# Matmuls in place of transposes as fillers of TensorE's first gaps

## The chip, the core and the metric

The kernel runs on one core of a Trainium2 chip. Its time is the device time in microseconds (us) of one execution, and of several executions the median is given. The engines are called by their short names: PE (TensorE, matmuls), ACT (ScalarE), DVE (VectorE), POOL (GpSimd) and SP, whose queue here issues the transfers.

## What is computed

Two parts in a row: a block-wise linear attention with decay, over 4 batches, 8 heads, 768 tokens and 64 dimensions, and a two-layer network with a leaky ReLU over the 3072 tokens of 512 features that come out of it.

```python
for b in range(nb):                       # blocks of 64 tokens
    qb, kb, vb = (q[:, :, sl], k[:, :, sl], v[:, :, sl])
    intra = np.einsum('bhic,bhjc->bhij', qb, kb) * Dmask[None]
    intra = np.einsum('bhij,bhjd->bhid', intra, vb)
    inter = np.einsum('bhid,bhde->bhie', qb * lam_pow[None], kv_state)
    out[:, :, sl] = intra + inter
    kb_dec = kb * rev_pow[None]
    kv_state = lam_block * kv_state + np.einsum('bhsd,bhse->bhde', kb_dec, vb)
...
x = attn_out.transpose(0, 2, 1, 3).reshape(B * S, H * D)     # 3072 x 512
h = x @ w_in                                                 # w_in 512 x 2048
return np.maximum(0.01 * h, h) @ w_out                       # w_out 2048 x 512
```

The weights `w_in` and `w_out` come as 64-bit floats and are turned into 32-bit ones on the chip.

## The kernel before

The tokens go in 24 chunks of 128 (`c`), and four chunks form a group of 512 (`g`). A chunk takes these steps: loads of k, q and v; transposes of k and q on PE against an identity (line 404) into PSUM, copied out by ACT (lines 415 and 416); the small 64x64 matmuls of scores, state and output (all in the helper `quad`, line 314); elementwise work on DVE and POOL between them (lines 420 to 463); and the split of the attention's output into three float32r parts, high, low and mixed (`xh`, `xl`, `xm`, lines 508 to 511). The three parts are held in `X[g % 2]`, so `X[1]` belongs to group 1 first. When a group is whole, the first layer multiplies it with the weights' three parts (`product`, line 641): 512-column float32r matmuls, four for each partial product. After all groups comes the second layer (line 701).

All work is added to a planner, `Plan`, with an engine, an estimated duration and the keys that it reads and writes. `emit` orders the operations by their estimated times and ranks, and then issues them in that order, so each engine's queue is fixed when the kernel is built. While it issues, `emit` also follows a second estimate of the time. Where PE would stand idle for more than 0.4 us by this estimate, it calls `self.idle(n)` with a number of fillers that is reckoned from the gap:

```python
if self.spare in self.ops[i][4]:
    self.idle = None
if self.idle is not None and t > soon[e] + 0.4:
    self.idle(int((t - soon[e] - 0.2) / 0.16))
```

It stops for good at the first operation that writes the bank `b10` (`spare`), which is the first 512-column matmul of the first layer. Until then the bank is free, and the fillers write their results there; nobody reads them. In the kernel before, `plan.idle` is `busy`: `n` transposes of the 128x128 identity with itself, in 32-bit floats (line 267). The same `busy` gives the eleven transposes that PE starts with (`WARM`), before the first data are there. The identity, `ident`, is made by POOL at the start. Fillers stand in PE's queue like other matmuls: what is behind them in the queue starts after them.

Of the kernel before, what the change touches and what calls it, by code (L numbers as in the profile page):

```python
# [31 lines left out]
def _bc(ap, idx, n):  # L32
    a = [list(x) for x in ap.ap]
    return bass.AP(ap.tensor, ap.offset, a[:idx] + [[0, n]] + a[idx:])
# [129 lines left out]
def kernel(  # L164
# [10 lines left out]
    nc = tc.nc  # L175
    P = 128
# [10 lines left out]
    T = GC * C  # L187
    WARM = 11
# [22 lines left out]
    def sb(shape, name, dt=F32):  # L211
        return pool.tile(shape, dt, name=name, tag=name)

    def ps(shape, name):
        return psum.tile(shape, F32, name=name, tag=name)
# [5 lines left out]
    b1, b2 = [ps([P, T], f"b1{i}") for i in range(2)], ps([P, T], "b2")  # L221
# [3 lines left out]
    X = [[sb([P, KO, T], f"x{x}{i}", F32R) for x in "hlm"] for i in range(2)]  # L225
# [14 lines left out]
    def part(n):  # L240
        nonlocal used
        used += n
        assert used <= NA, used
        return att[:, used - n:used]

    ident = part(P)
# [13 lines left out]

    nc.scalar.dma_start(out=lam_b, in_=lam.partition_broadcast(P))
    make_identity(nc, ident)

    def busy(n):

        for _ in range(n):
            nc.tensor.transpose(out=b1[0][:, 0:P], in_=ident, identity=ident)

    busy(WARM)
    nc.gpsimd.memset(zero, 0.0)  # L270
    plan = Plan()
    plan.idle, plan.spare, plan.warm = busy, "b10", 1.3 + 0.22 * WARM
    add = plan.add
    steady = False

# [546 lines left out]
```

## Time and profile before

| | us |
|---|---|
| median of three runs | 611.7 |
| runs | 611.04, 611.7, 614.07 |
| profiled execution, its time | 611.24 |
| profiled execution, its span | 609.4 |
| PE busy, share of the span | 598.5, 98% |
| DVE busy | 312.4 |
| ACT busy | 268.5 |
| POOL busy | 86.4 |

The span goes from the first to the last instruction of the profiled execution; its time holds some 2 us around it besides. PE's busy time contains matmuls that overlap: the record of one lasts longer than the distance to the next one. Lines such as L267 are those of the kernel before. In the kernel after, `busy` stands at line 269 and the new matmul at line 274, and all lines behind `hold` are 8 higher.

### The profile page before, as it was taken

What the parts mean: (1) busy time and instruction counts of PE and PEld (TensorE: products, weight loads), DVE (VectorE), ACT (ScalarE), POOL (GpSimd) and SP (SyncE); (2) the same over time, 40 slices, a digit from 0 to 9 for tenths busy, and PEclk for the clock granted to TensorE, in tenths of its full rate; (3) what the DMA queues carried; (4) which work ended last, traced back from release to release, by engine and by line L of the source; (5) the groups of instructions that cost most, each with busy time, mean ns of one, the idle gap of its engine ahead of it and who ended that gap; (6) DMA issues with size and microseconds to landing.
All of it is one profiled execution on the core that took longest, in us unless ns stands there. A gap on an engine that the chain in (4) does not pass through costs nothing.

```text
span 609.4 us, 12970 instructions
## 1 busy us (share of the span) xinstructions
PE 598.5 (98%) x5406; PEld 495.5 (81%) x5406; DVE 312.4 (51%) x417; ACT 268.5 (44%) x428; POOL 86.4 (14%) x91
## 2 busy tenths in 40 slices
PE   8899999999999999999999999999999999999997
PEld 6687888888888888888788888888888888888886
DVE  5899862434244326226366755545454544635531
ACT  4778884434465656565577522221222313214111
POOL 2753330314223004204000000000000000000000
PEclk9999999999999999999999999999999999999999
DMA  9999664767799877887686843424323332333201
GB/s 217 222 280 260 206 177 138 166 144 198 171 238 244 217 235 201 219 242 219 218 310 218 288 145 104 172 70 138 139 103 130 113 139 104 138 104 122 86 1 69
DMA packets 147754, 105.18 MB, mean 173 GB/s; under 512 B 123632, under 2 KB 124400, under 8 KB 147696
## 3 DMA queue, kind: packets, MB, share of 16 engines
q1 hardware_dynamic: 147552, 104.36, 57.9%
q8 instruction: 42, 0.69, 0.5%
q14 instruction: 16, 0.13, 0.1%
q10 hardware_dynamic: 144, 0.00, 0.0%
HBM read 68.69 MB, written 35.65 MB: 171 GB/s over the span
## 4 chain that ended last, share of the span: by engine, by line
PE 95%; DMA 2%; POOL 1%; DVE 1%; issue 0%; SPq 0%; ACT 0%; DVEq 0%; ACTq 0%
PE b L641 44%; PE b L701 18%; PE psc L701 11%; PE po L701 11%; PE po L314 4%; PE pt L701 4%; PE psc L314 3%; DMA att<-in_k_dram 1%; DMA att<-in_q_dram 1%; POOL att L420 1%; PE pt L404 1%; PE po L404 0%; SPq L339 0%; DVE wm L603 0%; PE b L404 0%
## 5 line engine op out<-in xcount | busy, mean ns | idle before, releaser
L683 ACT ACTIVATE xh<-att 128x1024 fp32r<-128x1024 f32 x48 | 50.7, 1060 | 149.0 <-PE b L701 140.7
L684 DVE SCALAR_TENSOR_TENSOR xl<-att,xh 128x1024 fp32r<-128x1024 f32 x48 | 58.6, 1223 | 97.7 <-ACT xh L683 97.7
L641 PE MATMUL b<-xh,wh 128*128 128x512 f32 (+1 forms) x392 | 102.9, 386 | 0.8 <-ACT xh L508 0.8
L641 PE MATMUL b<-xm,wm 128*128 128x512 f32 (+1 forms) x392 | 103.4, 391 | 0.0
L641 PE MATMUL b<-xl,wl 128*128 128x512 f32 (+1 forms) x392 | 102.8, 386 | 0.0
L641 PEld LDWEIGHTS b<-xh,wh 128*128 128x128 f32 x392 | 72.5, 188 | 15.9 <-ACT xh L508 1.0
L641 PEld LDWEIGHTS b<-xl,wl 128*128 128x128 f32 x392 | 72.5, 188 | 14.8
L659 ACT ACTIVATE b<-b 128x512 f32<-128x512 f32 x96 | 56.0, 584 | 63.1 <-PE b L641 63.0
L641 PEld LDWEIGHTS b<-xm,wm 128*128 128x128 f32 x392 | 71.0, 188 | 15.0 <-ACT b L659 0.4
L662 ACT ACTIVATE gs<-b 128x512 f32<-128x512 f32 x96 | 56.8, 598 | 41.6 <-PE b L641 38.4
L701 PE MATMUL b<-wh,xh 128*128 128x512 f32 x192 | 74.7, 389 | 0.0
L701 PE MATMUL b<-wl,xl 128*128 128x512 f32 x192 | 74.7, 389 | 0.0
L686 DVE SCALAR_TENSOR_TENSOR xm<-xl,xh 128x1024 fp32r<-128x1024 f32 x48 | 58.7, 1226 | 4.7
L701 PEld LDWEIGHTS b<-wl,xl 128*128 128x128 f32 x192 | 36.0, 188 | 7.5
L701 PEld LDWEIGHTS b<-wh,xh 128*128 128x128 f32 x192 | 36.0, 187 | 7.5
L453 DVE TENSOR_TENSOR att<-psc,att 128x512 f32<-128x512 f32 x24 | 16.5, 688 | 45.9 <-PE psc L314 45.8
L424 POOL TENSOR_TENSOR att<-att 128x512 f32<-128x512 f32 (+1 forms) x21 | 26.0, 1240 | 98.3 <-PE po L314 48.7
L420 POOL TENSOR_TENSOR att<-att 128x512 f32<-128x512 f32 (+1 forms) x23 | 29.8, 1294 | 64.2 <-DMA att<-in_k_dram 35.8
L585 DVE TENSOR_SCALAR w<-w 128x512 int32<-128x512 int32 x32 | 19.4, 605 | 36.9 <-ACT w L579 36.7
L701 PE MATMUL psc<-wh,xh 128*128 128x512 f32 x96 | 37.3, 389 | 0.0
L701 PE MATMUL psc<-wl,xl 128*128 128x512 f32 x96 | 37.3, 389 | 0.0
L701 PE MATMUL psc<-wm,xm 128*128 128x512 f32 x96 | 37.3, 389 | 0.0
(73 smaller groups left out, 810.1 us busy)
## 6 DMA issues: line engine op xcount, KB each, us to landing
att<-g SPq DMA_DIRECT2D x48, 512.0 KB, 3.2
g<-gs SPq DMA_DIRECT2D x47, 512.0 KB, 3.9
raw<-in_moe_w_in_dram SPq DMA_DIRECT2D x16, 512.0 KB, 5.3
raw<-in_moe_w_out_dram SPq DMA_DIRECT2D x16, 512.0 KB, 4.9
att<-in_k_dram SPq DMA_DIRECT2D x48, 128.0 KB, 3.8
att<-in_v_dram SPq DMA_DIRECT2D x24, 256.0 KB, 4.4
out_dram<-gs SPq DMA_DIRECT2D x23, 256.0 KB, 2.0
wo<-w SPq DMA_DIRECT2D x8, 512.0 KB, 5.9
```

The source lines that it names most:

```text
L314: nc.tensor.matmul(dst[HALF[cols]], lhsT=lhsT[HALF[rows]], rhs=rhs[HALF[rows]], start=start, stop=True, skip_group_check=True)
L420: lambda e="POOL": ENG[e].tensor_tensor(kr[nr], kr[nr], _bc(pow_k, 3, D)[nr], op=ALU.mult), ["fk"], [f"k{i}"])
L424: add(eng, us, lambda: e.tensor_tensor(o, x, _bc(pow_q, 2, 2)[:, :, m, :], op=ALU.mult), ["fq", dep], [f"qsT{i}"])
L453: add("DVE", 0.69, lambda: nc.vector.tensor_tensor(sc, psc[:, :, lower, :], decay, op=ALU.mult), ["psc", "fk"], ["sc"])
L585: add("DVE", 0.42, lambda: nc.vector.tensor_scalar(d, d, 3, None, op0=ALU.logical_shift_left), [], [key])
L641: nc.tensor.matmul(dst, lhsT=w[z][:, kk * 2 * P + f * P:kk * 2 * P + (f + 1) * P], rhs=x[z][:, kk, toks], start=start and kk == 0, stop=kk ...
L659: add("ACT", ns, lambda b=b: nc.scalar.activation(out=b, in_=b, func=AF.Copy, bias=0.0, scale=S + 1.0), [], [kb], rank=-1.5)
L662: add("ACT", ns, lambda b=b, r=r: nc.scalar.activation(out=r, in_=b, func=AF.Prelu, bias=0.0, scale=1.0 / WS, alpha=0.01), [kb], [f"gs{jg} ...
L683: add("ACT", 1.05, lambda: nc.scalar.activation(out=h, in_=graw[j], func=AF.Copy, bias=0.0, scale=NEAR), reads, wr("h"))
L684: add("DVE", 1.25, lambda: nc.vector.scalar_tensor_tensor(l, graw[j], 1.0, h.bitcast(F32), op0=ALU.mult, op1=ALU.subtract), reads + [f"rh{ ...
L686: add("DVE", 1.25, lambda: nc.vector.scalar_tensor_tensor(m, l.bitcast(F32), -S, h.bitcast(F32), op0=ALU.mult, op1=ALU.add), [f"rh{j}", f" ...
L701: nc.tensor.matmul(acc[tb][z // 2][:, cols], lhsT=ring[j][z][:, f * T + tb * P:f * T + (tb + 1) * P], rhs=W[pp][z][:, f * d_model:(f + 1) ...
```

## The change

A second identity, in float32r, is made at the start: ACT copies `ident` into the first 128 columns of the mixed part of `X[1]`. A new function `hold(n)` issues `n // 2` matmuls with this copy as the weights and the same copy, read four times in a row, as the 512 moving columns, into the whole bank `b10`, and one old transpose if `n` is odd. `plan.idle` becomes `hold`. The eleven transposes at the start stay as they are. The planner's estimates are the same, and so are the order of all other work and the places of the fillers.

```diff
     nc.scalar.dma_start(out=lam_b, in_=lam.partition_broadcast(P))
     make_identity(nc, ident)
+    idr = X[1][2][:, 0, 0:P]
+    nc.scalar.copy(idr, ident)
 
     def busy(n):
 
         for _ in range(n):
             nc.tensor.transpose(out=b1[0][:, 0:P], in_=ident, identity=ident)
+
+    def hold(n):
+
+        for _ in range(n // 2):
+            nc.tensor.matmul(b1[0], lhsT=idr, rhs=_bc(idr, 1, T // P), start=True, stop=True, skip_group_check=True)
+        busy(n % 2)
 
     busy(WARM)
     nc.gpsimd.memset(zero, 0.0)
     plan = Plan()
-    plan.idle, plan.spare, plan.warm = busy, "b10", 1.3 + 0.22 * WARM
+    plan.idle, plan.spare, plan.warm = hold, "b10", 1.3 + 0.22 * WARM
```

## The prediction

> **What bounds the kernel now.** I read the page first (busy shares, the forty slices, the chain), then the windows around the stage that holds the fillers, then the chain in order of time through that stage, and last the timeline of PE alone, group by group. From the page:
>
> ```profile
> span 609.4 us, 12970 instructions
> ...
> PE   8899999999999999999999999999999999999997
> ...
> PEclk9999999999999999999999999999999999999999
> ...
> PE 95%; DMA 2%; POOL 1%; DVE 1%; issue 0%; SPq 0%; ACT 0%; DVEq 0%; ACTq 0%
> ```
>
> TensorE carries 95% of the chain that ended last. Only the first two slices (15.2 us each) and the last are below 9 tenths. The windows (start:end, then stretch length, PE busy and its count, and so on) cut the span where the last filler ends:
>
> ```profile
> 5.00:31.00 26.00, 21.76 (x574) 16.73 (x573) 20.43 (x40) 16.80 (x30) 13.75 (x14) 1.00 1.02 238
> 31.00:609.50 578.50, 573.13 (x4820) 475.90 (x4820) 290.48 (x370) 250.40 (x397) 71.91 (x71) 1.00 0.56 170
> ```
>
> From 31 us on PE is busy for 573.13 of 578.50 us. The change leaves that work and its order as they are, so it can move the end only by moving the start of that stage. Before it, PE idles 26.00 - 21.76 = 4.24 us, and the fillers lie in such gaps. What sets the start of the long stage is the chain in order of time (start, duration, what), of which these are the pieces that matter, and one steady piece for scale:
>
> ```profile
> 2.34 3.45 DMA att<-in_q_dram
> ...
> 5.83 0.45 PE pt L404 x2
> ...
> 9.62 6.62 DMA att<-in_k_dram
> ...
> 16.29 0.82 PE b L404 x4
> ...
> 21.21 2.13 POOL att L420
> ...
> 28.42 0.59 PE b L267 x4
> 29.00 0.62 PE pt L404 x4
> ...
> 29.70 0.59 ACT att L416
> ...
> 30.84 1.21 PE b L641 x4
> ...
> 299.08 44.67 PE b L641 x196
> ```
>
> Up to 30 us the chain runs through loads, POOL, DVE and ACT, and returns to PE in short pieces. Of all the fillers that are exchanged, only one group (L267 x4 at 28.42) stands on it. A float32r matmul of 512 columns takes 44.67 / 196 = 0.228 us in the steady stage.
>
> **The fillers one by one.** The timeline of PE gives the groups (start, busy, line, count; in brackets the idle time ahead and who ended it). The L267 rows are the fillers; the row behind each shows when the work that they wait with went on:
>
> ```profile
> 1.36 2.61 PE L267 MATMUL b<-att 128*128 128x128 f32 x11 [1.36 <-POOL att L270]
> ...
> 5.05 0.49 PE L267 MATMUL b<-att 128*128 128x128 f32 x3
> 5.38 0.89 PE L404 MATMUL pt<-att 128*128 128x128 f32 x4
> 6.10 0.60 PE L267 MATMUL b<-att 128*128 128x128 f32 x4
> 6.94 0.69 PE L314 MATMUL psc<-att 64*64 64x64 f32 x32 [0.24 <-ACT att L416]
> ...
> 8.94 0.38 PE L267 MATMUL b<-att 128*128 128x128 f32 x2
> 9.33 0.93 PE L314 MATMUL po<-att 64*64 64x64 f32 x40
> ...
> 11.16 0.66 PE L267 MATMUL b<-att 128*128 128x128 f32 x4
> 12.67 1.16 PE L314 MATMUL psc<-att 64*64 64x64 f32 x64 [0.85 <-DVE att L460]
> ...
> 14.70 0.60 PE L267 MATMUL b<-att 128*128 128x128 f32 x4
> 15.23 0.93 PE L314 MATMUL po<-att 64*64 64x64 f32 x48
> ...
> 17.41 0.77 PE L267 MATMUL b<-att 128*128 128x128 f32 x5
> 18.51 1.16 PE L314 MATMUL psc<-att 64*64 64x64 f32 x64 [0.33 <-POOL att L420]
> ...
> 20.97 0.49 PE L267 MATMUL b<-att 128*128 128x128 f32 x3
> 21.39 0.93 PE L314 MATMUL po<-att 64*64 64x64 f32 x48
> ...
> 25.52 1.20 PE L267 MATMUL b<-att 128*128 128x128 f32 x9
> 27.49 0.93 PE L314 MATMUL po<-att 64*64 64x64 f32 x48 [0.76 <-DVE att L453]
> 28.35 0.66 PE L267 MATMUL b<-att 128*128 128x128 f32 x4
> 28.84 0.77 PE L404 MATMUL pt<-att 128*128 128x128 f32 x4
> ...
> 36.72 2.11 PE L641 MATMUL b<-xm,wm 128*128 128x512 f32 x8
> 38.66 1.98 PE L641 MATMUL b<-xh,wh 128*128 128x512 f32 x8
> ```
>
> The first eleven are the warm-up, which the change leaves as transposes. Counts behind them that are pairs or more: 3, 4, 2, 4, 4, 5, 3, 9 and 4; with one single filler, which stays a transpose, this makes 39. They turn into 17 matmuls of 512 columns and 5 transposes, 22 instructions.
>
> *Price of a pair.* Three transposes from 5.05 to 5.38 take 0.33 us, 0.11 each, so a pair is 0.22 us. A matmul of 512 columns is 0.228 us in the steady piece: +0.01 us a pair, 17 x 0.01 = +0.15 us of PE time in all if nothing else differs. At the head of a group behind the small 64x64 matmuls it may be more: eight L641 matmuls behind such work go from 36.72 to 38.66, 1.94 us, which is 0.12 us over 8 x 0.228; four transposes in the same place go from 28.35 to 28.84, 0.49 us, which is 0.05 us over 4 x 0.11. So a group behind small matmuls costs 0.07 us more at its head, and this holds for the groups of 11.16, 17.41, 25.52 and 28.35. The two ends of what a pair can cost are thus +0.01 and +0.08 us; I take +0.01 inside a group and +0.07 once at such a head.
>
> *What lies over it.* Group by group, what comes next anyway:
> - 5.05: the transposes of q behind it need a load that lands at 2.34 + 3.45 = 5.79. Two of them, 0.22 us from 5.38, would be through at 5.60. Cover 0.2 us against +0.01.
> - 6.10: the next small matmuls wait 0.24 us for ACT. Covered.
> - 8.94: from there to 9.33 are 0.39 us for two fillers of 0.22. Covered for +0.01.
> - 11.16, 17.41 and 25.52: idle of 0.85, 0.33 and 0.76 us remains behind the fillers, against +0.02 or +0.04 and the 0.07 at the head, at most 0.11 us. Covered three times.
> - 14.70: 0.53 us for four fillers of 0.44 and the change to small matmuls, so perhaps no idle; +0.02 us goes into the matmuls of 15.23. Behind them stands the load of k on the chain, landing at 9.62 + 6.62 = 16.24; the row at 15.23 with 0.93 us ends at 16.16. Cover about 0.1 us.
> - 20.97: +0.01 us, while the chain runs through POOL L420 from 21.21 for 2.13 us. Covered.
> - 28.35: on the chain. 0.02 + 0.07 = +0.09 us if nothing covers it. The four transposes of pt behind it should take 0.44 us, but their piece on the chain runs from 29.00 to 29.62 and ACT follows at 29.70. From 28.84 to 29.62 are 0.78 us; four transposes of 0.11 and the tail that the nine at 25.52 show (1.20 - 9 x 0.11 = 0.21) make 0.65. So 0.13 us of waiting lies there, for the load of q, and covers the 0.09.
>
> *The copy of the identity.* It is one ACT copy of 128x128, its wait is on the POOL work that the warm-up waits for too, and the first new filler waits for it in turn. Its bounds and its place, from the timeline of all engines:
>
> ```profile
> 1.20 1.28 ACT L415 ACT_TABLE_LOAD   x1 [1.20 <-PEq L806]
> ...
> 5.25 0.59 ACT L415 COPY att<-b 128x512 f32<-128x512 f32 x1 [2.77 <-PE b L404]
> ```
>
> ACT idles 2.77 us between 2.48 and 5.25. A copy four times as wide takes 0.59 us, so the new one ends by 3.07, and the first new filler is due at 5.05: 2 us of cover. Nothing else is behind it on ACT until 5.25. It lands in a tile that group 1 of the tokens fills much later; the queues of DVE, POOL and SP keep their instructions and waits.
>
> *The clock.* The eleven warm-up transposes take 2.61 / 11 = 0.24 us each, the nine at 25.52 take 1.20 / 9 = 0.13, and those from 5.05 on 0.11. So TensorE came to its full rate by 5.05 us, on nothing but transposes, and before the first filler that the change touches. From there to the end I see no slow stretch that other fillers could mend, so the gain from the clock is 0 in this execution. [...]
>
> *The sum.* Against the profiled execution, which took 611.24 us with a span of 609.4: 0 from the clock, 0 from the copy, 0 from eight groups, and between 0 and +0.09 us from the group at 28.35, of which I take 0. The profiled execution lies 0.46 us under the median of 611.7, inside the runs of 611.04 to 614.07. So I forecast the median itself: **611.7 us**, no change.
>
> **The rivals.**
>
> [...]
>
> [...]
>
> Third, *changing kinds costs more than the head of 0.07 us*, both into a group of float32r matmuls and out of it. With 0.1 us on each side of nine groups it is 1.8 us of PE time, of which the idle of 0.24, 0.85, 0.33 and 0.76 us covers four groups, and 5 x 0.2 = 1.0 us is left at most: 612.7.
>
> That the change doesn't do what it says: the copy comes late and the fillers begin with a wait. It would need ACT to be 2 us later than shown; I give it nothing of its own.
>
> **How the numbers follow.** No change beyond the covers: 0.66. First rival 0.13, of which 0.05 for over 0.5%. Second rival 0.11, of which 0.10 for over 0.5%. Third 0.10. A difference of 0.5% (3.06 us) is about what a measurement of this kernel can tell from no change. So faster 0.05, same 0.85, slower 0.10. The range: down to 610.0, which takes in the first rival with 1 us to spare for other runs of the same kernel, and up to 614.1, the highest run shown, which takes in the third; outside are the strong form of the first rival and most of the second.
>
> **What would show it.** In the profile after, the L267 groups of pairs give way to 17 matmuls of 128x512 that start at the same times within 0.1 us, the matmuls behind 6.94, 12.67, 18.51 and 27.49 still show idle ahead of them with the same releasers, and the first L641 work starts at 30.84 within 0.2 us (up to the jitter of the loads). ACT's copy stands between 2.4 and 3.1 us. I am wrong on the pair if a filler matmul takes over 0.25 us inside a group, on the cover if the first long matmuls begin over 0.5 us later with PE releasing ACT or DVE ahead of them, and on the clock if transposes or filler matmuls behind 5.05 us show twice their time, or show it before and not after.

## The result: 1.3 us less, from a place behind all the fillers

| | before | after |
|---|---|---|
| median of ten executions, us | 611.37 | 610.05 |
| range, us | 610.76 to 614.07 | 609.55 to 610.52 |
| profiled execution, us | 611.24 | 609.60 |
| its span, us | 609.4 | 607.8 |

The ratio is 0.997, with a 95% interval of 0.9956 to 0.9984. The forecast of no change put the median 1.65 us too high: 610.05 is at the low end of its range, and there is a small gain, clear of the noise. The ranges of the runs do not touch.

The page after says the same as the page before on the bounds:

```profile
span 607.8 us, 12937 instructions
...
PE 598.2 (98%) x5389; PEld 494.7 (81%) x5389; DVE 312.5 (51%) x417; ACT 268.3 (44%) x429; POOL 85.3 (14%) x91
...
PE 96%; DMA 3%; POOL 1%; ACT 0%; issue 0%; SPq 0%; DVE 0%; DVEq 0%; ACTq 0%
```

PE has 5389 matmuls in place of 5406, and "issue", time in which PE waits for nothing that the profile shows, is in the list of the chain with 0% in both: there a microsecond or two of 609 round to nothing. The stage with the fillers, in the timeline of PE after (start, busy, line, count, idle ahead):

```profile
4.92 0.78 PE L274 MATMUL b<-xm 128*128 128x512 f32 x1
5.50 0.40 PE L269 MATMUL b<-att 128*128 128x128 f32 x1
...
11.22 0.73 PE L274 MATMUL b<-xm 128*128 128x512 f32 x2
12.73 1.16 PE L322 MATMUL psc<-att 64*64 64x64 f32 x64 [0.78 <-DVE att L468]
...
24.85 1.20 PE L274 MATMUL b<-xm 128*128 128x512 f32 x4
25.88 0.27 PE L269 MATMUL b<-att 128*128 128x128 f32 x1
26.81 0.93 PE L322 MATMUL po<-att 64*64 64x64 f32 x48 [0.66 <-DVE att L461]
...
30.75 2.12 PE L649 MATMUL b<-xh,wh 128*128 128x512 f32 x8 [0.84 <-ACT xh L516]
```

The first long matmul starts at 30.75 us, before at 30.84. The covers held, and this stage gives 0.09 us of the 1.6 us that the spans differ by. The rest lies further on. The chain in order of time before (first fence) and after (second), around 55 us:

```profile
52.93 0.44 PE po L404 x4
53.37 0.44 PE pt L404 x4
53.80 0.86 PE po L314 x48
54.66 0.93 PE psc L314 x64
55.59 0.23 PE po L314 x13
55.82 1.41 issue
57.22 0.33 PE po L314 x3
57.55 7.17 PE b L641 x40
```

```profile
53.73 0.86 PE po L322 x48
54.58 0.93 PE psc L322 x64
55.52 0.23 PE po L322 x16
55.75 7.18 PE b L649 x40
```

Before, PE stops for 1.41 us behind the thirteenth of sixteen `po` matmuls, three short of the end of a round. It waits there for nothing that the profile shows: no semaphore, no load, no engine. After, the sixteen run through. At 52.93 the kernel after is 0.08 us ahead (52.85 there); at the long matmuls behind the round it is 1.80 us ahead. Of the 1.72 us between, the stall is 1.41, and the rest is the slower end of the round: 0.23 and 0.33 us for the sixteen `po` in two pieces, against 0.23 in one. Some 0.2 us are lost again further on, since the spans differ by 1.6. That one stall is the gain between the two profiles.

### The profile page after: what moved, and what is told of

The parts are those of the page before. It is cut to its first block, busy times and chain, and to the rows that moved or that the text cites. A ratio compares the mean times of both kernels' runs of the same rounds, so it can differ in the third digit from the quotient of the medians.

```text
span 607.8 us, 12937 instructions
## 1 busy us (share of the span) xinstructions
PE 598.2 (98%) x5389; PEld 494.7 (81%) x5389; DVE 312.5 (51%) x417; ACT 268.3 (44%) x429; POOL 85.3 (14%) x91
## 4 chain that ended last, share of the span: by engine, by line
PE 96%; DMA 3%; POOL 1%; ACT 0%; issue 0%; SPq 0%; DVE 0%; DVEq 0%; ACTq 0%
PE b L649 44%; PE b L709 18%; PE po L709 11%; PE psc L709 11%; PE po L322 4%; PE pt L709 4%; PE psc L322 3%; DMA att<-in_k_dram 2%; DMA att<-in_q_dram 1%; PE pt L412 1%; PE po L412 0%; PE b L412 0%; POOL att L428 0%; POOL att L471 0%; ACT att L424 0%
## 5 line engine op out<-in xcount | busy, mean ns | idle before, releaser
L432 POOL TENSOR_TENSOR att<-att 128x512 f32<-128x512 f32 (+1 forms) x21 | 26.0, 1238 | 97.1 <-DVE att L392 43.0
L471 POOL TENSOR_TENSOR att<-att 128x256 f32<-128x256 f32 x40 | 32.2, 805 | 38.9 <-DVE att L468 38.9
L709 PE MATMUL po<-wh,xh 128*128 128x512 f32 x96 | 37.3, 389 | 0.0
```

The source lines that it names most:

```text
L432: add(eng, us, lambda: e.tensor_tensor(o, x, _bc(pow_q, 2, 2)[:, :, m, :], op=ALU.mult), ["fq", dep], [f"qsT{i}"])
L471: add("POOL", 0.7, lambda new=new, j=j: nc.gpsimd.tensor_tensor(state[(j + 1) % 4], new, _bc(lam_c, 2, D), op=ALU.mult), [f"st{j % 4}", "f ...
L709: nc.tensor.matmul(acc[tb][z // 2][:, cols], lhsT=ring[j][z][:, f * T + tb * P:f * T + (tb + 1) * P], rhs=W[pp][z][:, f * d_model:(f + 1) ...
```

## The experiments

**What the stall is.** One line of the page gives the queue that brings the instructions:

```profile
q8 instruction: 42, 0.69, 0.5%
```

42 transfers of 16,384 bytes for 2 x 5406 matmuls and weight loads are 257 instructions for each. In the DMA view of before, cut to 54.88 to 55.83 us, one such block is under way, and none in the windows on both sides (53.50 to 54.88, 55.83 to 57.22):

```profile
q8 instruction: 1, 0.02, 6.1%
```

PE stops at 55.82 as it lands and goes on 1.4 us later. This gave theory A, an estimate of mine from these figures: PE's instructions come in blocks of 256; the next block is asked for late, and where PE runs through one block faster than the next can be had, it stands. The round's 128 small matmuls are, with their weight loads, just 256 instructions, and in the chain above the 125 ahead of the stall take 0.86 + 0.93 + 0.23 us, 2.0 us in all. By this theory the change, which takes 17 matmuls and 17 weight loads out ahead of this place, moves the end of the block away from it. Theory B was the other reading: the new kind of filler keeps the clock in executions that lose it.

**Half the old transposes.** The kernel before with

```diff
-    plan.idle, ... = busy, ...
+    plan.idle, ... = (lambda n: busy(n // 2 + n % 2)), ...
```

> The fillers are transposes as before, but half as many: 22 instead of 39, the same count of PE instructions as in the kernel after, and no copy of the identity. Theory A (instruction supply): what was won is the stall of 1.41 us at 55.8 us in the profile before, where PE waited for nothing but its own instructions; 17 matmuls and 17 weight loads fewer ahead of it move the place in the stream at which the next block of instructions is needed. By A this kernel is as fast as the one after, 610.1 us (609.7 to 610.6), and its profile shows no idle time put down to issue at 55 us. Theory B (kind of filler, clock): the float32r matmuls keep TensorE at its rate where transposes did not, in executions that no profile showed. By B this kernel is no faster than before, 611.4 us or more, since it has even less work in the gaps.

Measured: 609.48 to 609.83 us in seven executions with a granted clock (the mean share of TensorE's full rate over the execution) of 0.999 or 1, and 612.4 to 613.6 us in five with 0.993 to 0.997; over all twelve the ratio is 0.9988 (0.9969 to 1.0006). In its profile nothing is put down to issue at 55 us; the sixteen `po` run through:

```profile
54.66 0.93 PE psc L314 x64
55.60 0.23 PE po L314 x16
55.83 7.18 PE b L641 x40
```

So the gain needs no float32r filler and no copy of the identity: A. But five executions in twelve lost clock, which the ten of after did not. That B has a part too was not excluded.

**The new fillers, with the instructions of before.**

```diff
             nc.tensor.matmul(b1[0], lhsT=idr, rhs=_bc(idr, 1, T // P), ...)
+            if len(pads) < 8:
+                pads.append(nc.tensor.matmul(b1[0][0:64, 0:64], lhsT=ident[0:64, 0:64],
+                            rhs=ident[0:64, 0:64], start=True, stop=True, skip_group_check=True))
-        busy(n % 2)
+        busy(n % 2 + (n == 9))
```

> The kernel after, its 17 float32r fillers in place, with eight 64x64 float32 matmuls (each is two matmuls and two weight loads on PE) behind the first eight of them and one transpose more in the group of nine: 5406 matmuls as in the kernel before. Theory A (PE's instructions come in blocks of 256, and the block whose first instruction has 1967 matmuls and weight loads ahead of it is late when the block ahead of it is all small matmuls): the stall returns, 1.4 us of idle time put down to issue in the round behind 55 us, with 983 matmuls and 984 weight loads ahead of it, and executions at full clock take 611.4 us (610.9 to 612). If the stall went with the kind of filler, there is no idle time put down to issue, and the time is 610.1 us.

The stall is back at the same three matmuls (chain in order of time):

```profile
55.70 0.23 PE po L326 x13
55.93 1.56 issue
57.49 0.33 PE po L326 x3
57.82 7.19 PE b L653 x40
```

The profiled execution took 611.50 us, and the five lowest 610.9 to 611.6. The median is 613.06 us though (ratio 1.0021, 1.0002 to 1.0039), because six executions at full clock took 613.0 to 615.0. To catch one of them in a profile the kernel ran again.

> The kernel with the new fillers and 5406 matmuls once more. Of its twelve executions six at full clock took 613 to 615 us, 2 to 3 us over the five of 610.9 to 611.6, of which one was profiled. Theory A: if the profile falls on one of the slow six, it shows a second stall put down to issue, or a longer one, at another place with 1967 minus or plus a multiple of 1024 or of 256 PE instructions ahead of it. Otherwise (start of the long stage later, by the loads) the first 512-column matmul starts 2 us later than the 30.8 us of the other kernels. If it falls on one of the fast ones, it shows the stall of 1.4 to 1.6 us again.

That profile fell on the lowest time again, 611.15 us of 611.15 to 615.57, with 1.28 us of issue at the same place (ratio 1.0033, 1.0015 to 1.0051); the other six of its seven executions at full clock took 612.8 to 615.6 us. What the further 2 to 4 us of most executions are stays open: no profile shows one, and theory A does not give them.

**More instructions.** Two kernels with 64x64 matmuls added: one behind each of the 17 new fillers, and eight behind the warm-up of the kernel before.

```diff
             nc.tensor.matmul(b1[0], lhsT=idr, rhs=_bc(idr, 1, T // P), ...)
+            nc.tensor.matmul(b1[0][0:64, 0:64], lhsT=ident[0:64, 0:64], rhs=ident[0:64, 0:64], ...)
```

> The kernel after, with one 64x64 matmul behind each of the 17 new 512-column matmuls: the new kind of filler, but the instruction count of the kernel before. Theory A: the stall returns at the same place in the stream (three of the last po matmuls of the round that ends at 55.5 us in the profile after), 1.4 us of idle time put down to issue, and the time is 611.4 us (610.9 to 612). Theory B: the clock is kept as in the kernel after, 610.1 us.

```diff
     busy(WARM)
+    for _ in range(8):
+        nc.tensor.matmul(b1[0][0:64, 0:64], lhsT=ident[0:64, 0:64], rhs=ident[0:64, 0:64], ...)
```

> The kernel before, its old fillers, and eight 64x64 matmuls more behind the warm-up, in the wait for the first k. 16 PE instructions more than before. Theory A: the late block now begins 16 instructions earlier in the program, with more slow work in it, so 256 instructions take 3.2 us instead of 2.2 there and the stall shrinks from 1.4 to about 0.5 us: 610.6 us (610 to 611.2). Theory B: the same fillers and the same clock as before, so 611.4 us.

Both counted wrongly: such a float32 matmul is two matmuls and two weight loads on PE (the eight added are 16 in the timeline), so they had 5423 and 5422 matmuls, 34 and 16 PE instructions more than meant. Times: 613.1 to 622.7 us (ratio without the two longest 1.0059, 1.0036 to 1.0082) and 610.8 to 614.9 us (1.0016, 1.0003 to 1.003). As forecasts of a time both failed, and not by the clock alone, though five of ten and four of twelve executions lost some of it: at full clock the medians are 613.8 and 612.5 us, beside 611.6 for before in the same runs. These further microseconds stay open like those of the kernel with 5406 matmuls, which has added 64x64 matmuls too. Their profiles, of executions with a mean clock of 0.989 and 0.997, show something better: the stall follows the place in PE's stream and not the work. In the kernel with eight more it is 0.63 us long, near the 0.5 that A expected for 16 instructions, where 32 were added, and in the one with 17 more 0.91 (chains in order of time):

```profile
57.05 0.92 PE psc L316 x61
57.97 0.63 issue
```

```profile
66.50 0.92 PE psc L323 x60
67.42 0.91 issue
```

Here are the windows from the start to the end of each stall, with the counts of matmuls and weight loads begun until then: before, the kernel after with 5406 matmuls, the kernel before with eight more, and the one with 17 more, which has two stalls:

```profile
0.00:57.21 57.21, 50.14 (x983) 40.23 (x984) 47.09 (x80) 38.79 (x68) 25.12 (x28) 1.00 0.94 243
```

```profile
0.00:57.48 57.48, 51.61 (x983) 41.15 (x984) 47.91 (x81) 38.69 (x69) 25.23 (x28) 1.00 0.94 242
```

```profile
0.00:58.60 58.60, 51.70 (x983) 42.19 (x984) 45.39 (x78) 38.58 (x68) 22.67 (x28) 0.97 0.91 234
```

```profile
0.00:68.32 68.32, 64.06 (x983) 48.67 (x984) 45.86 (x78) 39.09 (x69) 23.80 (x28) 0.90 0.77 202
0.00:29.52 29.52, 26.89 (x476) 20.16 (x477) 17.67 (x40) 14.31 (x25) 10.03 (x17) 1.00 0.88 206
```

983 + 984 = 1967 each time, or 476 + 477 = 953. At 1967 it is the same round in all four: behind 13 of the last 16 `po` matmuls in the first two, and behind 61 and 60 of the 64 `psc` in the kernels with 16 and 17 matmuls more, just that many matmuls earlier in the work. In the kernel after, the same count is reached at 58.56 us, among long matmuls, with no idle time. Between the two counts lie 1014 matmuls and weight loads, and the trace has ten more PE instructions there that only wait: 1024, four blocks of 256.

**No fillers at all.**

```diff
-    plan.idle, ... = busy, ...
+    plan.idle, ... = (lambda n: None), ...
```

> No fillers at all in the gaps; the eleven transposes at the start stay. 39 matmuls and 39 weight loads fewer than before. Theory A: the block that was late before now ends in slow 512-column matmuls; the fastest stretch of 256 PE instructions between two needs takes 3.0 us at 283 us in place of 2.2, so no stall or at most some 0.5 us: 609.9 us (609.5 to 610.6), if the clock stays up without fillers. Theory B: without fillers the clock falls in a gap, 64x64 matmuls and transposes double in some stretch before 31 us, and the first long matmul starts some us later: 613 us or more.

609.7 to 614.0 us, median 612.31 (ratio 1.0003, 0.9986 to 1.002). The place of the stall was forecast wrongly: 1.5 us at 26 us, where a block ended inside the 64 `psc`, again with 953 instructions ahead:

```profile
25.23 1.15 PE psc L314 x61
26.38 1.50 issue
27.88 0.49 PE psc L314 x3
```

```profile
0.00:27.87 27.87, 20.41 (x476) 16.25 (x477) 18.24 (x41) 14.65 (x25) 11.44 (x18) 0.93 0.95 217
```

Its block is under way from 25.55 to 26.46 us in the DMA view: 2.3 us from its start until PE goes on. It is 2.3 us before (54.88 to 57.22), 2.4 in the kernel with 5406 matmuls (55.09 to 57.49) and 2.2 in the one with eight more (56.39 to 58.61).

These starts decide more than theory A says. With the blocks of 256 counted off from these places in the traces of before and after, PE enters every other block without a stall, and the transfer of each of these began 3.4 us or more ahead (the least is 3.45 us, for the one that PE enters at 14.70 us before); the speed of the block ahead tells less. In the kernel with 17 more, the 128 matmuls ahead of each stall, with their weight loads, took 5.3 and 5.6 us in its timeline (from 23.7 to 29.0 and from 61.8 to 67.4), and PE stood all the same. And in the kernel before another round of 128 small matmuls fills a block of its own, from 161.6 to 164.0 us, and is run through without a stall. Until its end 4767 matmuls and weight loads begin, 2800 more than until the end of the stall; with 16 that only wait, that is eleven blocks.

```profile
161.65 0.86 PE po L314 x48
162.51 0.95 PE psc L314 x64
...
163.69 13.87 PE b L641 x60
```

There the transfer of the block behind it had begun at 158.7 us, 5.3 us ahead. What sets the start of a transfer is not shown.

All twelve executions without fillers had a mean clock under 0.999 (0.988 to 0.997), and in the profiled one the first long matmul starts at 33.1 us. With the 39 transposes of before it was 22 of 96 executions (the table below), so without fillers the clock was lost more often, as B says of this kernel; the 613 us that it forecast came in four of the twelve.

**Eight transposes fewer.** The kernel before, with the group of nine cut to one:

```diff
-    plan.idle, ... = busy, ...
+    plan.idle, ... = (lambda n: busy(1 if n == 9 else n)), ...
```

> The kernel before with one change: the group of nine filler transposes at 25.5 us is one transpose. 16 PE instructions fewer than before, from a place behind which PE waits 0.76 us anyway. Theory A: the block that is late now starts 16 instructions later in the program; the 256 ahead of it then take 3.2 us in place of 2.2, so the stall of 1.4 to 1.6 us shrinks to about 0.5 us, in long matmuls instead of the last po matmuls, and executions at full clock take 610.3 us (610.0 to 610.8). If the stall has to do with the fillers themselves, it stays and they take 611.2 us. Theory B adds that the idle time of about 1.7 us that this leaves at 25.5 us costs the clock in more executions than the one in five of before.

Six executions at full clock took 609.9 to 611.2 us, with a median of 610.74; the 18 of before in the same runs had 611.77. Over all twelve, 611.13 us (ratio 0.9982, 0.9965 to 0.9998). The profile, of an execution that lost clock, shows no stall where 0.5 us was expected; the median of the six lies 0.7 and 0.95 us above those of the two sets of the kernel after, so in them a shorter one may be left. 16 instructions thus take away most of the stall or all of it, and the fillers were only their carrier. The other six lost clock, and the profiled one shows where, in the timeline of PE and in windows (the last three columns are clock, DMA share and GB/s):

```profile
25.31 0.33 PE L267 MATMUL b<-att 128*128 128x128 f32 x1
27.26 1.56 PE L314 MATMUL po<-att 64*64 64x64 f32 x48 [1.63 <-DVE att L453]
```

```profile
20.00:27.10 7.10, 4.87 (x143) 3.48 (x141) 6.59 (x8) 5.33 (x10) 6.02 (x5) 1.00 1.08 288
27.20:30.50 3.30, 3.24 (x56) 2.94 (x56) 3.16 (x7) 1.82 (x4) 2.30 (x3) 0.50 0.97 196
30.60:40.00 9.40, 8.56 (x114) 6.96 (x114) 8.31 (x11) 5.79 (x10) 3.92 (x3) 1.00 1.01 272
```

At the end of an idle time of 1.63 us the clock is 0.50, for 3.3 to 3.5 us by these windows, and then 1.00 again. In the 7.10 us just ahead of that PE is busy for 4.87. It does not fall each time: six executions of the same kernel had a mean clock of 0.999 or 1.

**Does the kind of filler matter to the clock?** The kernel after again, and with all 22 fillers of 512 columns:

```diff
-        for _ in range(n // 2):
+        for _ in range((n + 1) // 2):
             nc.tensor.matmul(b1[0], lhsT=idr, rhs=_bc(idr, 1, T // P), ...)
-        busy(n % 2)
```

> The kernel after once more, to count how often the clock is lost. Of the runs of before so far, 6 of 33 had a mean granted clock of 0.997 and took 612.4 to 614.0 us; of the ten of after none was under 0.999. Theory B (float32r matmuls of 512 columns keep the clock better than two transposes): again none or one of some 12 under 0.999, median 610.0 us. If the clock has nothing to do with the kind of filler, two of 12 are under 0.999 by the rate of before.

> The kernel after with the five odd transposes among its fillers turned into float32r matmuls of 512 columns too: 22 fillers, all of the new kind, the same count of PE instructions. Theory A: no stall put down to issue, executions at full clock 609.8 to 610.1 us. Theory B: none or one of 12 under a clock of 0.999. If the half transposes made the difference between the lowest times of the kernels, it is slower than after by the 0.1 us that five longer fillers cost at most.

609.86 us (ratio 0.9975, 0.9961 to 0.999) and 609.89 us (0.9956, 0.994 to 0.9973). And the kernel after with half the columns, twice, beside the half transposes once more ("the gate" in the expectations is whatever grants the clock; the runs show the granted clock alone):

```diff
-            nc.tensor.matmul(b1[0], lhsT=idr, rhs=_bc(idr, 1, T // P), ...)
+            nc.tensor.matmul(b1[0][:, 0:2 * P], lhsT=idr, rhs=_bc(idr, 1, 2), ...)
```

> The kernel after with 256 columns in place of 512 in each of the 17 new fillers: the same 22 filler instructions as in the kernel with half the transposes, about the same busy time (0.11 us each), and another kind for 17 of them. Of that one 5 of 12 executions lost clock (0.993 to 0.997, 612.4 to 613.6 us) and the others took 609.5 to 609.8 us. Theory B1, the gate goes by the kind: at most 2 of 12 lose clock, median 609.7 us. Theory B2, the gate goes by how long PE is busy, whatever the kind: some 5 of 12 lose clock again, lowest 609.5, the median between 609.7 and 612 us.

> The kernel with 256-column float32r fillers once more, for the count: 2 of 12 executions were under a clock of 0.999. Theory B1 (the kind counts): again at most two of 12. Theory B2 (the busy time counts): the same rate as the kernel with 22 transposes in this call. Executions at full clock 609.6 to 610.3 us.

> The kernel with 22 transposes as fillers (half of before) once more, for the count: 5 of 12 executions were under a clock of 0.999. Theory B1 (the kind counts): again about five of 12, clearly more than the kernel with 256-column float32r fillers. Theory B2 (the busy time counts): both kernels show the same rate, about four of 12. Executions at full clock 609.5 to 609.9 us.

610.01 us (0.9978, 0.9962 to 0.9995), 609.91 us (0.9964, 0.9948 to 0.998) and 610.07 us (0.9951, 0.9933 to 0.9969). Counted over all runs, by the mean granted clock of each execution:

| fillers | executions | under 0.999 | median of the others, us |
|---|---|---|---|
| 39 transposes (before, beside the kernels above) | 96 | 22 | 611.52 |
| 17 of 512 columns and 5 transposes (after, twice) | 22 | 1 | 609.79 to 610.05 |
| 22 of 512 columns | 8 | 0 | 609.89 |
| 22 transposes | 19 | 5 | 609.61 to 610.07 |
| 17 of 256 columns and 5 transposes | 24 | 4 | 609.83 to 609.84 |

At equal busy time the 512-column fillers of the table lose the clock in 1 of 30 and the transposes in 22 of 96; by chance alone that would come about once in a hundred times. But the kernels with 17 fillers of 512 columns and 64x64 matmuls added are not in the table: with 5406 matmuls 2 of 20 executions lost clock, and with 17 more 5 of 10, though B had expected the clock to be kept there. With them it is 8 of 60, which chance gives once in ten. At half the busy time, 4 of 24 against 5 of 19 tell nothing, the more so as the 5 all came in the first set and none of 7 in the second, where five of twelve had been expected. So it is not shown that the kind counts, and what it would be in the kind stays open. None of these kernels is clearly faster than the kernel after.

## Why the prediction was wrong

- *"It can move the end only by moving the start of that stage."* This is the step that failed. From 31 us on the work and its order are indeed the same, but not its place in PE's stream of instructions. The window from 31 us on had 578.50 - 573.13 = 5.37 us in which PE was not busy, and I did not ask what they were. Nor is that window all 512-column matmuls: rounds of 64x64 matmuls stand between them, and the stall lies in one. The waits of PE over the whole span, which I had read only up to 40 us, have it in the first row:

```profile
PE po L314 <- issue: 1.4, 1, 1.4
```

- *17 instructions fewer*, 34 with their weight loads. I named the smaller count, 22 for 39, and saw no gain in it. What it did was move the ends of the blocks: the 1967 matmuls and weight loads are through at 57.21 us before, inside a round, and at 58.56 after, among long matmuls. The term that I had at nothing is -1.4 us: 1.41 in the profile before, and 611.52 less 609.79 to 610.05, 1.5 to 1.7 us, between the medians at full clock.
- *The prices and covers of the fillers.* Right within 0.1 us: the first long matmul at 30.75 for 30.84, idle of 0.78 and 0.66 us left where 0.85 and 0.76 were, a copy of the identity that nobody waited for. The two new matmuls at 27.67 hold the transposes of `pt` at 28.24, 0.57 us, against the 0.49 + 0.09 = 0.58 of my terms, and the load of q covered it. (17 x 0.01 us is 0.17 and not 0.15; nothing hung on it.)
- *The clock.* I gave it 0 in the sum, and a chance of 0.13 to a gain by it and of 0.11 to a loss. What makes the clock fall, which these chances and the lower end of the range rest on, no run shows; in its place the runs showed how often it falls. In the profiled executions it was 0 (mean clocks of 1.000 and 0.999). Over all, 22 of 96 executions of before lost clock (of after 1 of 22); the 22 took 2.2 us longer than the others in the mean. In the mean over all that is 0.5 us, if other fillers were to lose none; in the median much less, since most executions keep it, and the measured median is 1.65 us under my forecast. No profile of before fell on such an execution. The one of the kernel with eight more did, with the mean clock of 0.997 that 21 of the 22 have: there the granted clock is 1.00 from 5 to 31 us and 0.98 from 31 to 100, and the first eight long matmuls, behind the last wait ahead of them (0.84 us), take 3.63 us from 31.70, where they take 2.13 before.
- *The third rival*, a loss at changes of kind, did not come.

The page of before had the figure that I needed: 42 instruction transfers, 257 of the 2 x 5406 matmuls and weight loads for each. The counts 1967 and 953 agree with blocks of 256: with the ten that only wait they are 1024 instructions apart. How many instructions PE holds ahead no run here measures. Had I laid the blocks over PE's stream, the block that is run through in 2.5 us, from 53.3 to 55.8, would have stood out as a place to ask about, though not yet as a stall: the one from 161.6 us is as fast and has none.

## What to carry to other kernels

Ask for the waits over the whole span, and take idle time put down to "issue" as a term: in this kernel (1.41 us before) it was, by the counts and the transfers, an engine that ran out of instructions, and it moves with the count of instructions ahead of it, however harmless the edit. Before a gain of some tenths of a per cent is credited to an idea, run the same count of instructions without the idea, and the idea with the old count. Where the clock comes and goes, count the executions that lose it, apart from the median of those that don't.

## What was unexpected of the hardware

PE's instructions came in 42 transfers, 257 matmuls and weight loads for each, and the counts ahead of the stalls lie 1024 instructions, four times 256, apart. Where PE ran out it went on 2.2 to 2.4 us after the transfer of the next block began; it stood for 0.5 to 1.6 us. A block of nearly nothing but 64x64 matmuls and their weight loads was used up in 2.4 to 2.5 us; PE then stood where the next transfer had begun 0.9 us ahead (54.88 for 55.82), and did not where it had begun 5.3 us ahead (158.7 for 164.0). At the end of one idle time of 1.63 us, in a stretch with smaller ones, the clock fell to 0.50 for 3.3 to 3.5 us in one execution, and six others of the same kernel had a mean clock of 0.999 or 1. With nothing but transposes on PE until then, one took 0.24 us at the start and 0.11 from 5.05 us on, but without any fillers in the gaps twelve of twelve executions lost some of the clock.
